# Sliding-window attention with a gated MLP on one core: the last row block stored in three pieces, the first chunk's softmax sums from one matmul, and a new order of the planned steps

## The chip, the cores and the metric

The kernel runs on one core of a Trainium2 chip. The metric is the device time of one execution in microseconds. A core has TensorE (PE, with its weight loads shown apart as PEld), VectorE (DVE), ScalarE (ACT), GpSimd (POOL) and SyncE (SP), and each engine takes its own instructions strictly in the order in which the program issued them.

## The reference

One transformer layer with pre-layernorm, sequence 2048, width 512, 32 heads of 16 columns, MLP width 1376, all in bf16:

```python
h  = x + A(layernorm(x));  h2 = h + B(layernorm(h))
# A: q,k,v = x @ wqkv;  each position s looks at s, s-2, ..., s-14 (8 places, those < 0 masked)
logits = einsum("bhsd,bhswd->bhsw", q, kg) * 16**-0.5
o = einsum("bhsw,bhswd->bhsd", softmax(logits), vg);  A = o @ wo
# B: gate = x @ W_gate; up = x @ W_up;  B = (relu(gate) * up) @ W_down
```

## The kernel before

The 2048 rows are cut into four chunks of 512 (`tk` 0 to 3), a chunk into four row blocks of 128. The work is written as 744 planned steps (`add(key, engine, ...)`). A chunk goes through these steps; the names below are the keys in the code, with the number of the part behind them:

- layernorm of x: `xst`, `xag` (statistics, DVE), `xxn` (normalised rows, on DVE or ACT), `xtp` (transposes, PE L531), `xte` (eviction, ACT L547), or a transposing DMA in place of the last two.
- q, k and v: 12 groups of four 128x512 matmuls (L572), each evicted on ACT (L580). In chunk 0 the first six groups come in pieces a, b (two matmuls of 256 columns each) and c (four).
- attention: `pr` products of q with shifted k (DVE, L620; in chunk 0 halves, L637), `sc` (16 matmuls, L628, summing over head columns), `ex` (exponent, ACT L696), in chunk 0 `mk` (masking the first columns, DVE L699). The eight places are in two halves, so there are `sc0`, `sc1`, `ex0`, `ex1`, `mk0`, `mk1`.
- softmax sums: `den` on PE, `dl` and `dr` on ACT (logarithm and exponent of its negative). In a chunk listed in `DEN1`, a DVE step `es` (L728) first adds the two halves and `den` is one matmul (L713); in the others `den` is two matmuls into one bank (L716). Chunks 1 to 3 then scale the weights (`am`, DVE L740); chunk 0 scales the result (`om`, DVE L795).
- `bd` spreads the weights over partitions by DMA from SP's queue (L756, four issues to a half), `mu` multiplies by shifted v (DVE L788, halves in chunk 0 L803), `ta` adds halves by an accumulating DMA from POOL's queue (L831), `tree2` and `tree1` add the rest (DVE L791, L825).
- `wo` output projection (L867), `rs` residual, layernorm of h (`hnm`, `hsq`, `hxn`, `htp`, `hte`).
- MLP: `mm` (up and gate, L940), evictions `ue` (L944) and `ge` (L947) on ACT, product `gu` (DVE L968), the last 96 columns apart (L907, L913, L917).
- `dn` down projection (L990), one step for `ft` 0 to 7 and one for `ft` 8 to 10; `o` adds the residual (DVE L1003, chunks 2 and 3), `os` stores (L1009; L1027 for chunks 0 and 1, whose residual is added by a DMA).

The order of the steps is written out by hand in a table `RANK`, one number for each step in the order of the `add` calls. `Plan.order` makes one queue of each engine, sorted by `RANK`, and never goes out of that order in a queue; the planner's durations only decide which buffer a step takes and in which order the engines' streams are written. So the table gives the order on each engine exactly. Buffers are few: 8 PSUM banks, 5 large tiles `big` for products, 9 tiles `quad`.

The down projection of the very last row block is cut into column pieces by `LASTC`, each with a bank, a DVE step and a store of its own; the store of the last piece listed goes through ACT's queue, the others through SP's:

```python
cs = (0,) + LASTC + (D,)
parts[-1:] = [(BPC - 1, a, b) for a, b in zip(cs, cs[1:])]
...
last = tk == NCK - 1 and n == len(parts) - 1
def f_os(j=j, c0=c0, c1=c1, ob=ob, tk=tk, q=nc.scalar if last else nc.sync):
    q.dma_start(out_rows[:, tk * BPC + j, c0:c1], ob.t[:, c0:c1])
```

Of the kernel before, what the change touches and what calls it, by code (L numbers as in the profile page):

```python
# [17 lines left out]
RANK = [  # L18
# [38 lines left out]
]  # L57


# [143 lines left out]
def kernel(  # L203
# [12 lines left out]
    Bsz, S, D = A_x.shape  # L216
# [5 lines left out]
    W = 8  # L222
    DIL = 2
    PADL = 16
    DEN1 = (1, 2, 3)
    BCD = {(0,0):"SSSS",(0,1):"SSSS",(1,0):"SSSS",(1,1):"SSSS",(2,0):"SSSS",(2,1):"SSSS",(3,0):"SSSS",(3,1):"SSSS"}
    PRE = ()
    PRD = ()
# [163 lines left out]
    HSP = ()  # L392
    TMT = (0, 1, 2, 3)
    TTM, DTG, ATE = 0.0845, 0.35, 0.3
    LASTC = (D // 2,)

    LNA = ((0, 1, 0, 1), (0, 0, 0, 0))

# [156 lines left out]
    for tk in range(NCK):  # L555
# [155 lines left out]
        def f_dn(exs=exs, dn=dn, tk=tk, es=None):  # L711
            if tk in DEN1:
                nc.tensor.matmul(dn.t[:], lhsT=(same if tk in EARLY else spread)[:], rhs=es.t[:], start=True, stop=True)  # L713
                return
            for hf in range(2):
                nc.tensor.matmul(dn.t[:], lhsT=(same if tk in EARLY else spread)[:], rhs=exs[hf].t[:], start=(hf == 0), stop=(hf == 1))  # L716
# [6 lines left out]

        if tk in DEN1:
            es = Buf(es_s)
# [250 lines left out]
        if tk == NCK - 1:  # L976
            cs = (0,) + LASTC + (D,)
            parts[-1:] = [(BPC - 1, a, b) for a, b in zip(cs, cs[1:])]
# [98 lines left out]
```

## Time and profile before

| what | value |
| --- | --- |
| three timed runs | 196.38, 196.60, 196.94 us; median 196.6 |
| the profiled execution, whole time | 196.0 us |
| its span in the trace | 193.7 us (2.3 us lie around it) |
| granted TensorE clock, mean | 1.00 |
| busy: PE, DVE, ACT, POOL | 188.5, 147.2, 115.2, 17.4 us |

The profile is of one execution, 0.6 us under the median of the timed runs. Times in its rows count from the start of the span. A line of the timeline gives start, length, engine, source line, operation, what it writes and reads, and in brackets the idle time before it and who ended it. Matmuls are pipelined, so one 128x512 matmul is shown as 379 ns long while the next starts about 216 ns after it. About one matmul record in sixty is missing; the weight loads are all there, and serve to place the steps.

### The profile page before, as it was taken

What the parts mean: (1) busy time and instruction counts of PE and PEld (TensorE: products, weight loads), DVE (VectorE), ACT (ScalarE), POOL (GpSimd) and SP (SyncE); (2) the same over time, 40 slices, a digit from 0 to 9 for tenths busy, and PEclk for the clock granted to TensorE, in tenths of its full rate; (3) what the DMA queues carried; (4) which work ended last, traced back from release to release, by engine and by line L of the source; (5) the groups of instructions that cost most, each with busy time, mean ns of one, the idle gap of its engine ahead of it and who ended that gap; (6) DMA issues with size and microseconds to landing.
All of it is one profiled execution on the core that took longest, in us unless ns stands there. A gap on an engine that the chain in (4) does not pass through costs nothing.

```text
span 193.7 us, 3083 instructions
## 1 busy us (share of the span) xinstructions
PE 188.5 (97%) x1120; PEld 99.0 (51%) x1139; DVE 147.2 (76%) x239; ACT 115.2 (59%) x241; POOL 17.4 (9%) x35
## 2 busy tenths in 40 slices
PE   7999999999999999999999999999999999999993
PEld 7986455555436435454444554444445444545452
DVE  6889999999999999999997679999564401134331
ACT  3489898965999673965156649623478712435500
POOL 3000002330000013100044001003000000000000
PEclk9999999999999999999999999999999999999999
DMA  6799564999902609917579974135101624001102
GB/s 205 242 296 376 138 155 93 192 196 260 353 5 49 171 14 199 191 33 170 122 143 194 180 192 90 29 80 94 18 0 27 162 58 135 0 27 54 30 23 86
DMA packets 25070, 24.61 MB, mean 127 GB/s; under 512 B 11136, under 2 KB 21344, under 8 KB 25056
## 3 DMA queue, kind: packets, MB, share of 16 engines
q1 hardware_dynamic: 22032, 16.23, 30.1%
q0 software_dynamic: 2304, 7.34, 20.8%
q10 hardware_dynamic: 720, 0.85, 1.2%
q8 instruction: 9, 0.15, 0.3%
q14 instruction: 5, 0.04, 0.1%
HBM read 8.42 MB, written 2.10 MB: 54 GB/s over the span
## 4 chain that ended last, share of the span: by engine, by line
PE 97%; ACT 1%; issue 1%; DVE 0%; ACTq 0%
PE bank L940 35%; PE bank L572 21%; PE bank L990 20%; PE bank L867 7%; PE bank L628 4%; PE bank L421 3%; PE bank L907 3%; PE bank L531 2%; PE bank L429 1%; ACT up_sb L944 1%; PE bank L870 0%; PE bank L713 0%; PE bank L716 0%; DVE row L1003 0%; ACT vT L580 0%
## 5 line engine op out<-in xcount | busy, mean ns | idle before, releaser
L940 PE MATMUL bank<-quad,wgu_sb 128*128 128x512 bf16 x312 | 72.4, 379 | 0.4
L940 PEld LDWEIGHTS <-wgu_sb 128*128 128x128 bf16 x320 | 31.0, 98 | 36.4 <-issue 1.0
L990 PE MATMUL bank<-wd_sb,gT 128*128 128x512 bf16 (+2 forms) x185 | 39.6, 366 | 0.1
L944 ACT CAST up_sb<-bank 128x512 bf16<-128x512 f32 x40 | 22.3, 590 | 22.2 <-PE bank L940 20.5
L572 PE MATMUL bank<-quad,wqk_sb 128*128 128x512 bf16 (+1 forms) x148 | 29.4, 344 | 0.3
L947 ACT ACTIVATE gr<-bank 128x512 bf16<-128x512 f32 x40 | 23.5, 606 | 9.5 <-PE bank L940 5.2
L968 DVE TENSOR_TENSOR gT<-gr,up_sb 128x1024 bf16<-128x1024 bf16 x20 | 13.8, 688 | 19.4 <-ACT up_sb L944 10.5
L990 PEld LDWEIGHTS <-gT 128*128 128x128 bf16 (+1 forms) x187 | 18.2, 98 | 19.8 <-DVE gT L968 0.2
L620 DVE TENSOR_TENSOR big<-quad,kT 128x4096 bf16<-128x4096 bf16 x12 | 27.2, 2284 | 0.2 <-ACT kT L580 0.2
L788 DVE TENSOR_TENSOR big<-big,vT 128x4096 bf16<-128x4096 bf16 x12 | 27.1, 2285 | 0.2 <-PE bank L940 0.2
L572 PEld LDWEIGHTS <-wqk_sb 128*128 128x128 bf16 x152 | 16.7, 113 | 10.3 <-issue 0.2
L831 POOL DMA_DIRECT2D big<-big x12 | 10.5, 904 | 81.7 <-DVE big L788 54.2
L791 DVE TENSOR_TENSOR big<-big 128x1024 bf16<-128x1024 bf16 (+2 forms) x24 | 16.9, 728 | 0.0
L572 PE MATMUL bank<-quad,wv_sb 128*128 128x512 bf16 x61 | 15.3, 380 | 0.2
L867 PE MATMUL bank<-wo_sb,quad 128*128 128x512 bf16 x62 | 15.0, 379 | 0.1
L1003 DVE TENSOR_TENSOR row<-x_sm,bank 128x512 bf16<-128x512 bf16 (+1 forms) x9 | 5.5, 627 | 12.2 <-PE bank L990 12.2
L456 ACT ACTIVATE row<-x_sm,mv 128x512 bf16<-128x512 bf16 x12 | 8.6, 718 | 7.2 <-DVE mv L448 7.1
L547 ACT COPY quad<-bank 128x1024 bf16<-128x1024 bf16 (+1 forms) x10 | 8.6, 898 | 7.2 <-PE bank L531 7.2
L878 DVE SCALAR_TENSOR_TENSOR x_sm<-x_sm,bank 128x512 bf16<-128x512 bf16 x12 | 8.2, 687 | 4.9 <-PE bank L867 4.7
L580 ACT CAST kT<-bank 128x512 bf16<-128x512 f32 x16 | 9.1, 597 | 3.3 <-PE bank L572 1.8
L467 DVE BATCH_NORM_STATS2 st<-x_sm 128x6 f32<-128x512 bf16 x16 | 10.2, 675 | 0.4 <-DMA x_sm<-in_A_x_dram 0.4
L580 ACT CAST quad<-bank 128x512 bf16<-128x512 f32 x16 | 9.5, 602 | 1.6 <-PE bank L572 1.5
(77 smaller groups left out, 169.5 us busy)
## 6 DMA issues: line engine op xcount, KB each, us to landing
big<-big POOLq DMA_DIRECT2D x12, 512.0 KB, 5.3
big<-ex SPq DMA_DIRECT2D x32, 128.0 KB, 2.8
wgu_sb<-in_B_W_gate_dram SPq DMA_DIRECT2D x2, 688.0 KB, 7.7
wgu_sb<-in_B_W_up_dram SPq DMA_DIRECT2D x2, 688.0 KB, 7.5
wd_sb<-in_B_W_down_dram SPq DMA_DIRECT2D x2, 640.0 KB, 7.9
x_sm<-in_A_x_dram SPq DMA_DIRECT2D x2, 512.0 KB, 5.1
x_sm<-up_sb POOLq DMA_DIRECT2D x4, 256.0 KB, 3.8
out_dram<-x_sm SPq DMA_DIRECT2D x4, 256.0 KB, 2.3
```

The source lines that it names most:

```text
L572: nc.tensor.matmul(mm.t[:, lo:hi], lhsT=wv_sb[:, dt, t:D:NT] if c == 2 else wqk_sb[:, dt, c * D + t:(c + 1) * D:NT], rhs=xnT.t[:, dt, lo:h ...
L580: nc.scalar.copy(out=o, in_=mm.t[:])
L620: V.tensor_tensor(out=pb.t[:].rearrange("p (t w) s -> p t w s", t=2), in0=q4, in1=k4, op=ALU.mult)
L788: V.tensor_tensor(out=mt.t[:], in0=ab.t[:], in1=v8, op=ALU.mult)
L791: V.tensor_tensor(out=mt.t[:, 0:n, :], in0=mt.t[:, 0:n, :], in1=mt.t[:, n:2 * n, :], op=ALU.add)
L831: nc.gpsimd.dma_start(mt.t[:, 0:4, :], mt.t[:, 4:8, :], accum_op=ALU.add)
L867: nc.tensor.matmul(od.t[:], lhsT=OT.t[:, t, j * P:(j + 1) * P], rhs=wo_sb[:, t, :], start=(t == 0), stop=(t == NT - 1 and tk not in RPE))
L940: nc.tensor.matmul(mm.t[:fs, lo:hi], lhsT=wgu_sb[:, dt, g, ft * P: ft * P + fs], rhs=hnT.t[:, dt, lo:hi], start=(dt == 0), stop=(dt == NT ...
L944: nc.scalar.copy(out=ub.t[:fs, i, :], in_=um.t[:fs, :])
L947: nc.scalar.activation(out=gr.t[:fs, i, :], in_=gm.t[:fs, :], func=ACT.Relu)
L968: V.tensor_tensor(out=gt.t[:fs, 0:n, :], in0=gr.t[:fs, 0:n, :], in1=ub.t[:fs, 0:n, :], op=ALU.mult)
L990: nc.tensor.matmul(od.t[:, c0:c1], lhsT=gts[ft].t[:fs, ft % 2, j * P:(j + 1) * P], rhs=wd_sb[:fs, ft, c0:c1], start=(ft == 0), stop=(ft == ...
```

## The change

Three things are changed.

1. `LASTC` goes from (256,) to (256, 384): the last row block's output is made in pieces of 256, 128 and 128 columns instead of 256 and 256. The number of planned steps rises by four (two `dn`, one `o`, one `os`).
2. `DEN1` takes in chunk 0: one DVE step `es` more, one 128x512 matmul less in `den` of chunk 0.
3. `RANK` is a new table with 749 numbers.

```diff
 RANK = [
     0, 1, 2, 3, 4, 5, 6, 7, 8, 9, 10, 11, 12, 13, 14, 15, 16, 17, 18, 19,
     20, 22, 23, 25, 29, 31, 32, 21, 24, 26, 28, 30, 36, 39, 40, 27, 33, 35, 37, 42,
-    47, 51, 34, 38, 41, 43, 46, 50, 55, 44, 56, 69, 77, 64, 65, 76, 79, 48, 53, 60,
...
+    45, 49, 34, 38, 41, 43, 46, 50, 54, 64, 73, 75, 78, 65, 67, 70, 81, 47, 56, 58,
...
-    DEN1 = (1, 2, 3)
+    DEN1 = (0, 1, 2, 3)
...
-    LASTC = (D // 2,)
+    LASTC = (D // 2, 3 * D // 4)
```

Put against the `add` calls, the two tables read as follows in the places of which the prediction speaks (chunk behind the dot; q0a is piece a of group q0; dn3a, dn3b, dn3c are the column pieces of the last row block):

```
PE, start, before: xtp0.0 fill xtp1.0 fill q0a k1a xtp2.0 q1a xtp3.0 k1b q1b q0b k2a q1c k1c ...
PE, start, after:  xtp0.0 fill xtp1.0 fill k1a xtp2.0 q1a xtp3.0 k1b q2a k2a q1b q1c k1c ...
DVE, chunk 0, before: seven half products, mk1.0, the eighth, xst.3, mk0.0, xst.2, xag.2, mu1c.0 ...
DVE, chunk 0, after:  eight half products, mk1.0, xst.3, mk0.0, xst.2, xag.2 with es.0, mu1c.0 ...
PE, up to wo1.1: the same 117 steps in both tables, den.0 shorter by one matmul after
DVE, up to tree1_1.1 (the last before wo1.1): 112 steps before; the same and es.0 after
PE, end, before: dn0lo dn1lo dn2lo dn0hi dn1hi dn2hi dn3b dn3a
PE, end, after:  dn0lo dn3b(lo) dn1lo dn0hi dn1hi dn3b(hi) dn2lo dn2hi dn3a dn3c
SP, end, before: (transpose of chunk 3) os0.3 os2.3 os1.3 os3a.3          ACT: os3b.3
SP, end, after:  (transpose of chunk 3) os1.2 os2.2 os0.2 os3b.3 os0.3 os1.0 os3.2 os1.3 os2.3 os3a.3   ACT: os3c.3
```

70 rows, old and new, of the table RANK are left out of this document.

## The prediction

> **What bounds the kernel now.** I read the head of the page first, then the chain of work that ended last, then who waited for whom.
>
> ```profile
> span 193.7 us, 3083 instructions
> ...
> PE 188.5 (97%) x1120; PEld 99.0 (51%) x1139; DVE 147.2 (76%) x239; ACT 115.2 (59%) x241; POOL 17.4 (9%) x35
> ...
> PE   7999999999999999999999999999999999999993
> ...
> DVE  6889999999999999999997679999564401134331
> ...
> PE 97%; ACT 1%; issue 1%; DVE 0%; ACTq 0%
> ```
>
> PE is busy in every slice and carries 97% of the chain. The list of waits, cut to PE, has one entry, for the first warm-up matmul:
>
> ```profile
> PE bank L421 <- DVE warm L322: 1.0, 1, 1.0
> ```
>
> So from 1.0 us to the last down projection PE never visibly stands still: the kernel is bound by PE's count of matmuls, and an order can gain nothing in this execution by filling PE's gaps. But the slices show DVE at 9 tenths from 12 us to some 100 us as well. Added up over that part:
>
> ```profile
> core 0: us, PE busy (x) PEld busy (x) DVE busy (x) ACT busy (x) POOL busy (x), PEclk, DMA share, GB/s
> ...
> sum 74.00, PE 73.44 PEld 37.80 DVE 72.91 ACT 58.46 POOL 8.03; mean PE 12.24 PEld 6.30 DVE 12.15 ACT 9.74 POOL 1.34
> ```
>
> Between 12 and 86 us DVE is idle for 1.1 us of 74, hardly more than PE. Where the two meet decides whether a saving on PE reaches the end. They meet here (timeline around 84 to 86 us):
>
> ```profile
> 83.64 0.68 DVE L968 TENSOR_TENSOR gT<-gr,up_sb 128x1024 bf16<-128x1024 bf16 x1
> ...
> 84.38 1.55 PEld L990 LDWEIGHTS <-gT 128*128 128x128 bf16 x8 [0.17 <-DVE gT L968]
> 84.54 1.89 PE L990 MATMUL bank<-wd_sb,gT 128*128 128x512 bf16 x8
> ...
> 85.63 0.43 DVE L825 TENSOR_TENSOR quad<-big 128x512 bf16<-128x512 bf16 x1
> ...
> 86.05 0.96 PEld L867 LDWEIGHTS <-quad 128*128 128x128 bf16 x5
> ...
> 86.26 1.03 PE L867 MATMUL bank<-wo_sb,quad 128*128 128x512 bf16 x4
> ```
>
> Chunk 0's first down projection loads its weights at 84.38, and the gated product it needs ends at 84.32 (83.64 + 0.68). Chunk 1's first output projection `wo1.1` loads at 86.05, and the last `tree1` ends at 86.06. PE goes straight on at 86.26, so it loses nothing yet, but its spare time there lies between 0 (by the weight load) and 0.2 us (by the matmul).
>
> **The change part by part.** *Chunk 0's softmax sums.* The two matmuls are this piece of the chain, and the price of the DVE step is read from an operation of the same shape on two 128x512 bf16 tiles and the start behind it:
>
> ```profile
> 29.48 0.43 PE bank L716 x2
> ...
> 59.78 0.42 DVE L740 TENSOR_TENSOR ex<-ex,rec 128x512 bf16<-128x512 bf16 x1 [0.34 <-ACT rec L722]
> 60.13 0.41 DVE L502 TENSOR_SCALAR row<-x_sm,mv,rs 128x512 bf16<-128x512 bf16 x1
> ```
>
> PE: one of two goes, 0.43 / 2 = 0.22 less. DVE: `es.0` adds 60.13 - 59.78 = 0.35. Behind `es.0` in DVE's queue stand the `mu` steps of chunk 0, and so everything up to 86 us.
>
> *The start.* Before, four matmuls of 256 columns stand ahead of the third block's transposes; after, two.
>
> ```profile
> 8.22 0.73 DVE L502 TENSOR_SCALAR row<-x_sm,mv,rs 128x512 bf16<-128x512 bf16 x2
> ...
> 8.46 0.60 PE L572 MATMUL bank<-quad,wqk_sb 128*128 128x256 bf16 x4
> ...
> 8.89 0.39 PE L531 MATMUL bank<-identity,row 128*128 128x128 bf16 x4
> ```
>
> PE would be at the transposes at 8.46 + 0.22 = 8.68. Their input is the first of the two L502, which ends at 8.63 (8.22 and the 0.41 that one takes above). With some 0.1 us from DVE to PE the transposes start at about 8.75, so PE loses 0.0 to 0.15; I take 0.08. The piece `k1c`, which with `q1c` releases DVE's first product, now has one piece less ahead of it (0.22) and that loss, so DVE's dense stretch starts 0.14 earlier.
>
> *The meeting at `wo1.1`.* In both tables PE's queue up to it holds the same 117 steps, and DVE's queue up to the last `tree1` the same steps with `es.0` added. So PE comes there 0.22 - 0.08 = 0.14 earlier, and DVE 0.35 - 0.14 = 0.21 later if its waits stay as they are: 0.35 to be covered by 0 to 0.2 of spare time. PE stalls 0.15 to 0.35; with shorter DVE waits, 0. I take 0.15, by the matmul row, since that is what counts on PE. PE then comes away from there at -0.14 + 0.15 = +0.01: the matmul saved is given back to DVE.
>
> *After 86 us* PE alone is the bound, and the next margins, from the rows below, are 0.35 (121.08 - 120.73) at chunk 1's down projection and 0.42 (180.73 - 180.31) at chunk 3's.
>
> ```profile
> 120.05 0.68 DVE L968 TENSOR_TENSOR gT<-gr,up_sb 128x1024 bf16<-128x1024 bf16 x1
> ...
> 121.08 0.31 PEld L990 LDWEIGHTS <-gT 128*128 128x128 bf16 x2
> ...
> 179.62 0.69 DVE L968 TENSOR_TENSOR gT<-gr,up_sb 128x1024 bf16<-128x1024 bf16 x1 [1.15 <-ACT gr L947]
> ...
> 180.73 2.47 PEld L990 LDWEIGHTS <-gT 128*128 128x128 bf16 x12
> ...
> L947 ACT ACTIVATE gr<-bank 128x512 bf16<-128x512 f32 x40 | 23.5, 606 | 9.5 <-PE bank L940 5.2
> ```
>
> In the new table the product for the first stands ahead of a long `mu`. For the second, the last gate group that it needs has three groups of four matmuls (12 x 0.216 = 2.6) between itself and the down projection, and two evictions and a product (2 x 0.61 + 0.69 = 1.9) to wait for. Both margins get wider. Cost 0.
>
> *The end.* Rows of the timeline, then of the groups by shape, the chain in order of time (start, length) and the DMA issues (KB, us to landing):
>
> ```profile
> 188.74 1.92 PE L990 MATMUL bank<-wd_sb,gT 128*128 128x256 bf16 x16
> 189.94 0.35 ACTq L1009 DMA_DIRECT2D out_dram<-row  x1
> 190.69 0.42 DVE L1003 TENSOR_TENSOR row<-x_sm,bank 128x256 bf16<-128x256 bf16 x1 [0.78 <-PE bank L990]
> 191.14 0.33 SPq L1009 DMA_DIRECT2D out_dram<-row  x1
> ...
> L1003 DVE TENSOR_TENSOR row<-x_sm,bank 128x512 bf16<-128x512 bf16 x7 | 4.6, 686 | 10.9 <-PE bank L990 10.9
> ...
> 61.05 0.89 PE bank L531 x16
> ...
> out_dram<-row ACTq DMA_DIRECT2D x1, 64.0 KB, 1.6
> out_dram<-row SPq DMA_DIRECT2D x1, 64.0 KB, 1.5
> ```
>
> A 256-column matmul costs (1.92 - 0.27) / 15 = 0.11 us, the 0.27 being the overhang of the last one. A 128-column one is bounded by 0.89 / 16 = 0.056 (transposes, each with a weight load of its own) and 0.11; I take 0.056. Before 22 x 0.11 = 2.42, after 11 x 0.11 + 22 x 0.056 = 2.44: +0.02. The last DVE step shrinks: 512 columns take 0.69, 256 take 0.42, so 128 should take 0.42 - 0.13 = 0.29: -0.13. The last store has half the bytes (saves up to 0.1) and goes by ACT's queue instead of SP's (1.6 against 1.5, costs 0.1): 0, between -0.1 and +0.1. ACT has nothing else left by then. SP now has seven stores to issue in the last 4 us, about 0.35 each, 2.5 in all; the one that it issues last (`os3a`) may go out 0.6 before the piece `dn3c` ends on DVE. Hidden.
>
> The pieces of 128 columns rest on the transposes' row. [...]
>
> The pieces' stores write rows of 256 bytes, where before they were 512. [...]
>
> *Sum:* 0.01 (PE up to 86 us, softmax sums included) + 0.02 - 0.13 + 0 = -0.10. The profiled execution took 196.0 for its 193.7 of span, and would take 195.9. The timed runs' median stands 0.6 above it at 196.6; the same difference gives 196.5.
>
> **The rivals.**
>
> *The order takes away DVE's waits, and stalls of the timed runs (faster).* For it: all three timed runs (196.38 to 196.94) lie above the profiled one, and at 84 to 86 us PE has no spare time, so any later transfer that holds DVE up stalls PE one for one. If the new order absorbs that, the 0.22 of the matmul and the 0.13 of the end come through and about 0.4 of the 0.6 goes: 196.6 - 0.35 - 0.4 = 195.85. Against it: DVE has only 1.1 us of idle time to give, and the runs' distance may be no stall at all.
>
> *DVE comes later still (slower).* In DVE's queue of chunk 0 `mk1` moves behind the eighth half product. SP's spreading of the weights waits for it, and `mu1c` waits for that:
>
> ```profile
> 20.21 0.16 DVE L699 TENSOR_TENSOR ex<-ex,mask 128x16 bf16<-128x16 bf16 x1
> 20.28 1.22 DVE L637 TENSOR_TENSOR big<-quad,kT 128x2048 bf16<-128x2048 bf16 x1
> ...
> 20.39 6.14 SPq L756 DMA_DIRECT2D big<-ex  x8
> ...
> 26.97 1.23 DVE L803 TENSOR_TENSOR big<-big,vT 128x2048 bf16<-128x2048 bf16 x1
> ...
> DMA to landing us min/median/max: 2.7/3.2/4.7
> ```
>
> A half product takes 1.1 from start to start, so the issues start 1.1 - 0.14 = 1.0 later, the fourth at about 20.39 + 3 x 0.77 + 1.0 = 23.7 (6.14 / 8 = 0.77 an issue). With the slowest landing (4.7) it is there at 28.4; the same sum for before gives 27.4, though `mu1c` ran at 26.97, so 28.0 is nearer. `mu1c` is due at 26.97 + 0.35 - 0.14 = 27.2. DVE would lose 0.8, which reaches PE at `wo1.1`: 196.5 + 0.8 = 197.3. It decides from 0.7 us of such lateness on. Against it: with the median landing (3.2) the data are there at 26.9, in time.
>
> *Narrow matmuls wait for their weights (slower).* A weight load is shown as 98 ns long, so if it is not hidden, the end costs 22 x (0.098 - 0.056) = 0.9 more: 197.4. The transposes speak against it.
>
> ```profile
> L990 PEld LDWEIGHTS <-gT 128*128 128x128 bf16 x170 | 16.6, 98 | 17.9 <-DVE gT L968 0.2
> ```
>
> **How the numbers follow.** 0.3% is 0.6 us, about what these runs can tell from no change. The forecast, 196.5 with a range of its own from 196.0 to 197.1 (0 to 0.35 of stall, 0.1 either way at the store, 0.2 of spread in the medians), has 53 in 100 and lies within 0.3%. The faster rival has 24, late DVE 18, bare weight loads 5. So faster 0.24, same 0.53, slower 0.23. The range 195.7 to 197.5 leaves out the far part of the faster rival (some 7 in 100) and of the slower ones (some 10).
>
> **What the profile after would show.** Right: PE's only wait is again the warm-up; one L713 with 0.22 in place of two L716; PE's last matmul within 0.2 us of where it was; a last L1003 of 128 columns at about 0.29; DVE busy over 98% up to `wo1.1`, whose weight load is released by DVE. Wrong: a DVE idle time of over 0.5 before the first L803; PE's wait for L825 over 0.4 at `wo1.1`, or none with DVE done well ahead of it; steps of over 0.08 between the 128-column matmuls; a last landing of over 1.8 us.

## The result, and the profile after

The change made the kernel slower by 0.7%: a median of 197.69 us (ten runs, 197.11 to 199.18) against 196.54 for the kernel before (ten runs, 195.98 to 196.94), a ratio of 1.0068 with a 95% interval of 1.0045 to 1.0090. The forecast was 196.5 with a range from 195.7 to 197.5; the case "slower by over 0.3%" had been given 0.23. The profiled execution took 197.51 for a span of 195.7 (1.8 around it; before 196.0, 193.7 and 2.3). Ratios here leave out executions over 1.5% longer than the fastest of their kernel (five of twelve in e6, four in e5), medians hold all, so the two can differ.

The page of the kernel after: busy time, slices of PE and DVE, and the chain by engine.

```profile
span 195.7 us, 3123 instructions
...
PE 188.9 (97%) x1149; PEld 98.3 (50%) x1149; DVE 147.8 (76%) x241; ACT 114.6 (59%) x241; POOL 17.0 (9%) x35
...
PE   7699999999899999999999999999999999999993
...
DVE  6699999999899989999997669999683504121432
...
PE 73%; DVE 15%; DMA 5%; issue 2%; ACT 2%; SPq 2%; DVEq 0%; ACTq 0%
```

PE's share of the chain has gone from 97% to 73%, though its busy share of the span stays at 97%: the chain now runs through DVE up to the last place where PE waits for it. The list of waits says where, cut to PE (us in total, times, longest):

```profile
PE bank L531 <- DVE row L502: 1.4, 1, 1.4
PE bank L421 <- DVE warm L322: 1.0, 1, 1.0
PE bank L867 <- ACT kT L580: 0.6, 1, 0.6
PE bank L572 <- ACT rs L480: 0.3, 1, 0.3
PE bank L867 <- DVE quad L825: 0.2, 1, 0.2
```

Before, the warm-up's entry was the only one. Four places lose time now; three of them stand in this list (the start twice), the one at 34 us in the timeline alone. The first is the start (timeline):

```profile
6.98 0.69 DVE L467 BATCH_NORM_STATS2 st<-x_sm 128x6 f32<-128x512 bf16 x1 [1.78 <-DMA x_sm<-in_A_x_dram]
...
8.04 0.40 PE L531 MATMUL bank<-identity,row 128*128 128x128 bf16 x4 [1.39 <-DVE row L502]
...
9.33 0.38 PE L572 MATMUL bank<-quad,wqk_sb 128*128 128x256 bf16 x2 [0.33 <-ACT rs L480]
```

x's third row block lands late, its statistics stand in DVE's queue ahead of the second block's normalising, and PE's first q or k matmul starts at 9.33, not at 8.46. In the kernel before, DVE's longest wait for these loads was:

```profile
DVE st L467 <- DMA x_sm<-in_A_x_dram: 0.4, 1, 0.4
```

The second is at 34 us, behind SP's queue:

```profile
25.49 2.50 SPq L756 DMA_DIRECT2D big<-ex  x4
...
28.08 5.25 SPq L520 DMA_TRANSPOSE quad<-row  x4
28.19 2.36 DVE L803 TENSOR_TENSOR big<-big,vT 128x2048 bf16<-128x2048 bf16 x2 [0.22 <-DMA big<-ex]
...
33.88 0.83 PE L531 MATMUL bank<-identity,row 128*128 128x128 bf16 x12
...
34.80 0.58 PEld L572 LDWEIGHTS <-wqk_sb 128*128 128x128 bf16 x4 [0.26 <-issue]
34.83 1.03 PE L572 MATMUL bank<-quad,wqk_sb 128*128 128x512 bf16 x4
```

By an estimate from the profile before (0.89 / 16 = 0.056 for each of 16 transposes) these twelve are done after 12 x 0.056 = 0.67, at 34.55; the next matmul starts at 34.83, a loss of 0.28. It needs chunk 3's rows, which come by the transposing DMAs, and these stand behind the spreading of the weights on SP. This profile names no releaser there (`issue`); the lists of e4 and e5 name that DMA (`quad<-row`), with 0.4 and 0.9. The kernel before issued both some 1.45 earlier; 0.87 of that is its earlier start, which moves PE as well, and about 0.6 is left for the order:

```profile
24.04 2.49 SPq L756 DMA_DIRECT2D big<-ex  x4
26.62 3.92 SPq L520 DMA_TRANSPOSE quad<-row  x3
```

The third is at 51 us, the fourth at `wo1.1`:

```profile
48.52 2.29 DVE L620 TENSOR_TENSOR big<-quad,kT 128x4096 bf16<-128x4096 bf16 x1
49.08 0.81 PE L572 MATMUL bank<-quad,wqk_sb 128*128 128x512 bf16 x3
...
50.59 0.38 PE L870 MATMUL bank<-x_sm,identity 128*128 128x512 bf16 x1
...
50.89 1.07 ACT L580 CAST kT<-bank 128x512 bf16<-128x512 f32 x2 [4.20 <-DVE big L620]
51.51 2.29 DVE L620 TENSOR_TENSOR big<-quad,kT 128x4096 bf16<-128x4096 bf16 x1 [0.71 <-ACT kT L580]
51.52 1.02 PE L867 MATMUL bank<-wo_sb,quad 128*128 128x512 bf16 x4 [0.56 <-ACT kT L580]
```

```profile
87.67 0.38 PE L867 MATMUL bank<-wo_sb,quad 128*128 128x512 bf16 x1
87.81 0.42 DVE L825 TENSOR_TENSOR quad<-big 128x512 bf16<-128x512 bf16 x1
...
88.29 0.76 PEld L867 LDWEIGHTS <-quad 128*128 128x128 bf16 x5 [0.73 <-DVE quad L825]
88.29 1.04 PE L867 MATMUL bank<-wo_sb,quad 128*128 128x512 bf16 x4 [0.24 <-DVE quad L825]
```

At 50.89 ACT evicts chunk 3's k block of t = 2 (`k2ev.3`). Its matmuls are the last ones ahead of the output projections, and its bank is full at 49.89 (49.08 + 0.81). For most of the 4.2 us that ACT stands still it waits for them; for the last 1.0 it waits for DVE's product `pr0t2.1` to end (48.52 + 2.29 = 50.81). That product reads chunk 1's part of k blocks 2 and 3 in one instruction, and from the first address to the last it spans chunk 3's part of block 2, which the eviction writes. In the table before, the matmuls of that k block stand 13 places earlier in PE's queue. With ACT held, PE gets no bank for `wo2.0` (51.52 - 50.59 - 0.22 = 0.72 lost), and DVE's next product waits 0.71 for the eviction. At `wo1.1` DVE comes late with the last `tree1`, and PE's second matmul starts at 88.29, 0.62 after the first, where the four from 88.29 on start 0.22 apart (1.04 less the 0.38 of the last, by 3): 0.40 lost. That the held eviction makes this fourth stall too is not shown: e5 and e18 below have it without the third.

From its first q or k matmul to the end of its last matmul PE takes 182.19 us before (8.46 to 190.65) and 183.18 after (9.33 to 192.51). The three stalls make 0.28 + 0.72 + 0.40 = 1.40, the matmul saved takes 0.22 off, and the end (below) adds 0.03: 1.21 for the 0.99 measured, so that 0.22 stays unexplained.

The end, in the timeline:

```profile
192.54 0.29 DVE L1003 TENSOR_TENSOR row<-x_sm,bank 128x128 bf16<-128x128 bf16 x1 [0.20 <-PE bank L990]
192.86 0.36 ACTq L1009 DMA_DIRECT2D out_dram<-row  x1
```

The DMA issues (KB each, us to landing), then the chain's last piece (start, length) in the kernel after and in the kernel before:

```profile
out_dram<-row ACTq DMA_DIRECT2D x1, 32.0 KB, 1.5
```

```profile
182.93 9.59 PE bank L990 x66
```

```profile
181.11 9.56 PE bank L990 x55
```

Eleven matmuls more cost 0.03, the last DVE step takes 0.29 in place of 0.42, and the last store lands after 1.5.

### The profile page after: what moved, and what is told of

Its sections match the earlier page's. It is cut to its first block, busy times and chain, and to the rows that moved or that the text cites. A ratio compares the mean times of both kernels' runs of the same rounds, so it can differ in the third digit from the quotient of the medians.

```text
span 195.7 us, 3123 instructions
## 1 busy us (share of the span) xinstructions
PE 188.9 (97%) x1149; PEld 98.3 (50%) x1149; DVE 147.8 (76%) x241; ACT 114.6 (59%) x241; POOL 17.0 (9%) x35
## 4 chain that ended last, share of the span: by engine, by line
PE 73%; DVE 15%; DMA 5%; issue 2%; ACT 2%; SPq 2%; DVEq 0%; ACTq 0%
PE bank L940 26%; PE bank L990 19%; PE bank L572 14%; PE bank L867 7%; DVE big L620 5%; DVE big L788 4%; PE bank L628 3%; DMA x_sm<-in_A_x_dram 3%; DVE big L791 2%; PE bank L907 2%; PE bank L531 2%; DMA big<-ex 2%; DVE gT L968 1%; SPq L756 1%; DVE quad L825 1%
## 5 line engine op out<-in xcount | busy, mean ns | idle before, releaser
L990 PE MATMUL bank<-wd_sb,gT 128*128 128x512 bf16 (+4 forms) x198 | 39.9, 356 | 0.0
L944 ACT CAST up_sb<-bank 128x512 bf16<-128x512 f32 x40 | 22.9, 597 | 16.1 <-PE bank L940 14.3
L572 PE MATMUL bank<-quad,wv_sb 128*128 128x512 bf16 x64 | 16.0, 381 | 0.0
L1003 DVE TENSOR_TENSOR row<-x_sm,bank 128x512 bf16<-128x512 bf16 (+2 forms) x10 | 5.7, 579 | 8.2 <-PE bank L990 7.9
L547 ACT COPY quad<-bank 128x1024 bf16<-128x1024 bf16 (+1 forms) x10 | 8.7, 891 | 5.3 <-PE bank L531 5.3
L502 DVE TENSOR_SCALAR row<-x_sm,mv,rs 128x512 bf16<-128x512 bf16 x24 | 8.7, 407 | 3.1 <-ACT rs L484 3.1
```

What stands on the lines that cost most here:

```text
L572: nc.tensor.matmul(mm.t[:, lo:hi], lhsT=wv_sb[:, dt, t:D:NT] if c == 2 else wqk_sb[:, dt, c * D + t:(c + 1) * D:NT], rhs=xnT.t[:, dt, lo:h ...
L944: nc.scalar.copy(out=ub.t[:fs, i, :], in_=um.t[:fs, :])
L990: nc.tensor.matmul(od.t[:, c0:c1], lhsT=gts[ft].t[:fs, ft % 2, j * P:(j + 1) * P], rhs=wd_sb[:fs, ft, c0:c1], start=(ft == 0), stop=(ft == ...
```

## The experiments

PE's part is the time from its first q or k matmul to the end of its last matmul, so that a late start doesn't count; the profiled execution alone shows it. In brackets stands the median of the kernel before, run in turn with that row's kernel; e7, e8 and e12 to e14 follow in the text.

| kernel | median us (before) | 95% interval of the ratio | PE's part | first q/k matmul |
| --- | --- | --- | --- | --- |
| before | | | 182.19 | 8.46 |
| after | 197.69 (196.54) | 1.0045 to 1.0090 | 183.18 | 9.33 |
| e1 | 198.47 (196.75) | 1.0049 to 1.0113 | 183.35 | 9.46 |
| e2 | 196.88 (196.75) | 0.9990 to 1.0044 | 183.51 | 7.93 |
| e3 | 196.34 (196.75) | 0.9950 to 1.0002 | 182.43 | 8.90 |
| e4 | 197.29 (196.75) | 0.9993 to 1.0049 | 183.67 | 8.65 |
| e5 | 197.56 (196.57) | 0.9963 to 1.0028 | 183.18 | 9.26 |
| e6 | 197.29 (196.57) | 0.9956 to 1.0013 | 181.86 | 8.26 |
| e9 | 197.15 (196.61) | 1.0006 to 1.0068 | 183.42 | 8.51 |
| e10 | 196.88 (196.61) | 1.0000 to 1.0071 | 184.35 | 8.35 |
| e11 | 196.64 (196.61) | 0.9972 to 1.0031 | 183.03 | 8.98 |
| e15 | 197.28 (196.75) | 1.0010 to 1.0074 | 183.64 | 8.75 |
| e16 | 196.55 (196.75) | 0.9969 to 1.0016 | 182.64 | 9.07 |
| e17 | 196.22 (196.71) | 0.9947 to 0.9997 | 182.44 | 8.78 |
| e18 | 197.33 (196.71) | 0.9990 to 1.0057 | 182.58 | 8.51 |

**The three parts one by one (e1 to e4).** e1 takes the new order alone, e2 the one matmul for chunk 0's sums alone, e3 the three pieces alone, e4 is the kernel after again.

```diff
 e1, from after:  DEN1 and LASTC as before; RANK: without es.0, the last row block's steps as before
 e2, from before: DEN1 = (0, 1, 2, 3); RANK: es.0 behind xag3.2
 e3, from before: LASTC = (D // 2, 3 * D // 4); RANK: the last row block's steps in the new order
```

> The new order alone: after's table without the step es of chunk 0, den of chunk 0 as two matmuls, the last row block in pieces of 256 and 256 with the end of before's table. Theory O (the order itself makes stalls: the eviction of k to the last chunk held behind a product on DVE, a late spreading of the weights): 197.3 to 198.0, ratio about 1.006 as the whole change, with PE's wait of 0.6 for ACT's L580 near 50 us again. Theory D (the softmax step on DVE, 0.35 at the place where DVE holds PE): 196.5 to 196.8. Theory S (the profiled run of after merely had late input loads): 196.5, no PE wait between 12 and 86 us.

> Before's order with chunk 0's softmax sums from one matmul, es behind the statistics of chunk 2 on DVE as in the new table. Theory O: 196.3 to 196.8, since at most 0.35 of DVE less 0.2 of spare time reaches PE and 0.22 of matmul goes. Theory D: 196.9 to 197.4, with a PE wait for L825 of over 0.3 at the first output projection of chunk 1. My prediction's step: a stall of 0.15 (0 to 0.35) there, PE's end within 0.1 of before's.

> Before's order with the last row block in 256, 128 and 128 columns and the new table's order of chunk 3's last steps. All theories: 196.4 (a tenth less), between 196.2 and 196.7; steps of 0.056 between the 128-column matmuls, the last DVE step 0.29. If narrow matmuls wait for their weights or the 256-byte rows land late: 196.9 to 197.4.

> The changed kernel once more, with a second profile. Theory O: 197.4 to 198.2, and the waits near 50 us (PE for ACT's L580) and near 70 us (DVE for the spread weights) are there again. Theory S: where the input loads land as early as in the profile of before (third block by 5.6 us), the span is within 0.5 us of before's 193.7.

The order alone gives 1.0081, and the intervals of e2 and e3 hold 1: the order carries the loss. e3's profile has no wait on PE but the warm-up's, and its time from PE's last matmul to the end of the span is 2.81, against 3.05 before. e2 saves nothing that can be measured; in its profile x's chunk 1 was late and cost PE 1.0 near 17 us, and PE has no wait for L825 in it. e1, without `es.0`, does stall at `wo1.1`, by 0.34 (88.07 to 88.63, less 0.22): the order makes that stall without `es.0` as well. e4 has the same stalls as the profile after (0.53 at 34, 0.71 at 51, 0.46 at 87 us), at a smaller distance to the kernel before; its interval, 0.9993 to 1.0049, holds 1.

**The held eviction (e5, e6).** e5 makes chunk 1's products of q and k in two instructions, one to a k block, so that none spans another chunk's columns. e6 leaves them and moves chunk 3's k block.

```diff
 e5, from after:  chunk 1's L620 in two halves: kT block t, then block t + 1
 e6, from after:
-PE: k2mm.3 where the table has it            ACT: k2ev.3 likewise
+PE: k2mm.3 behind sc1.1                      ACT: k2ev.3 behind ex1.1
```

> The changed kernel with chunk 1's products of q and k as two DVE instructions to a step, one for each column block t, instead of one over two blocks; nothing else. Theory K (the 4.2 us for which ACT stands before its L580 at 50.9 us is the eviction of k's block 2 of chunk 3 held back behind DVE's product, because that one instruction spans the rows between its two blocks): ACT's eviction starts when its matmuls end, near 49.8; PE's wait of 0.5 to 0.7 near 51.5 and DVE's of 0.7 there go; DVE pays 4 x 0.07 = 0.3 for the splits; 0.4 to 0.9 us faster than after in the same rounds. Theory B (a PSUM bank or a q buffer holds the eviction): the wait of about 4.2 stays, time as after or 0.3 more.

> The changed kernel with the projection of k's block 2 of chunk 3 moved on PE from before the first output projection to behind the second score step of chunk 1 (sc1), and its eviction on ACT from before rs0 of chunk 0 to behind ex1 of chunk 1. Theory K: PE's wait near 51.5 goes and DVE's 0.7 at the product before it, 0.6 to 1.2 us faster than after, and the wait at the first output projection of chunk 1 near 88 us shrinks from 0.4 below 0.2. Theory B: the wait comes back at another eviction, time within 0.3 of after.

Who waits for whom, first e5, then e6, cut to PE and to the evictions into kT:

```profile
ACT kT L580 <- PE bank L572: 3.2, 1, 3.2
...
PE bank L421 <- DVE warm L322: 1.0, 1, 1.0
...
PE bank L572 <- DMA quad<-row: 0.9, 1, 0.9
...
PE bank L876 <- DVE quad L834: 0.2, 1, 0.2
```

```profile
PE bank L421 <- DVE warm L322: 1.0, 1, 1.0
...
ACT kT L580 <- PE bank L572: 0.7, 1, 0.7
...
PE bank L572 <- ACT rs L480: 0.3, 1, 0.3
```

With the product split, ACT waits for PE's matmuls only and PE's wait at 51 us is gone: it is the one instruction's span over two blocks that made the dependency. In e5 the transposes of chunk 3 cost 0.9 instead, the stall at `wo1.1` is there with 0.34, PE's part is that of the kernel after, and the gain that was expected isn't shown. In e6 the stalls at 51 and at 87 us are both gone, and PE's part is the shortest of all. Its timed runs fell into two groups (195.07 to 197.46 and 198.45 to 199.03), so it was run again:

> e6's kernel a second time (the order after, chunk 3's k block of t = 2 moved behind sc1.1 and ex1.1). If the held-back eviction and what followed from it (0.72 and 0.40 on PE) are the larger part of the loss: 1.1 less than the kernel after's 197.3 to 197.7, so 196.2 to 196.6, ratio 0.998 to 1.001, and no PE wait over 0.3 between 40 and 100 us. Rival (something outside of PE's waits makes the new order slow): 197.2 or more, as the kernel after.

In e18 the wait at 51 us is absent again and PE's part is 0.6 below that of the kernel after, but the stall at `wo1.1` is there with 0.46, and the runs spread from 195.8 to 201.3. So with that k block moved PE's part is 0.6 to 1.3 shorter than in the kernel after; that moving it suffices is not shown.

**The mask and the start (e7, e8).** Both come from the kernel after.

```diff
 e7: DVE: mk1.0 ahead of the eighth half product
 e8: DVE: xxn1.0 ahead of xst2.0, xte1.0 ahead of xst3.0
```

> The changed kernel with mk1 of chunk 0 ahead of the eighth half product on DVE, as before the change. If the late spreading of the weights causes PE's wait of 0.3 to 0.5 near 34.5 us (the transposing DMAs of chunk 3 stand behind it in SP's queue), this wait falls under 0.1 and DVE's wait of 0.2 to 1.1 before its first L803 too: 0.3 to 0.8 us faster than after. If not, within 0.2 of after.

> The changed kernel with two DVE steps of the start moved up: the normalisation of row block 1 ahead of the statistics of row block 2, and the copy of block 1's transposes ahead of the statistics of block 3. Theory S (part of the time comes from DVE waiting in order for late rows of x): the first L572 starts at or before 8.6 us also where the third row block lands after 6 us; 0.3 to 0.8 us faster than after, and the spread of the runs is smaller. Otherwise within 0.2 of after.

e7: 197.89, ratio 1.0061 (1.0034 to 1.0088). Its profile caught an execution in which x's chunk 1 was 2.3 late at 19 us; the wait at 34 us is gone in it, but PE was held 2.3 ahead of that place, so this doesn't show that the mask's place causes the wait. DVE's `mk1.0` waits 1.1 for the exponent in it, which the late x may have caused. The gain of 0.3 to 0.8 that was expected did not come. e8: 198.20, 1.0088 (1.0059 to 1.0118). PE's first q or k matmul comes at 7.78, and then PE waits 0.81 for the third row block and 0.94 at 19 us: the wait only moved, and here too the expected gain did not come.

**Heads crossed (e9 to e12).** A table's first 111 or 114 steps, up to chunk 0's last product or mask, joined to the rest of the other. e11 adds e6's edit to e9; e12 is e2 and e3 together.

```diff
 e9,  after:  RANK = before's first 111 steps, then the others in after's order
 e10, before: RANK = after's first 114 steps, then the others in before's order
```

> The kernel after, with the first 111 steps (everything up to chunk 0's last half product, about the first 30 us) in the order of the kernel before, and the rest in the order of the kernel after. Theory A (the order's own waits): the start's loss of about 0.8 to 1.2 us goes (x's third row block at 5.3 to 5.7 us, first L572 near 7.2), the wait for the k eviction near 51 us (0.7) and the stall at wo1.1 (0.3 to 0.45) stay: 197.3 to 197.7 of the kernel after less 0.9, so 196.4 to 196.8. Rival B (x's lateness is luck and has nothing to do with the order): the third row block lands anywhere between 5.4 and 7.1, and the median stays at 197.3 to 197.7.

> The kernel before, with the first 114 steps (up to chunk 0's second mask) in the order of the kernel after; two matmuls for chunk 0's denominators, two pieces at the end. Theory A: x's third row block lands at 6 us or later, PE's matmuls start 0.5 to 1.2 later, nothing else changes: 196.6 + 0.9 = 197.5. Rival B: 196.6, with a start as in the kernel before or not, by luck.

> As e9, and with chunk 3's k block of t = 2 moved behind sc1.1 on PE and its eviction behind ex1.1 on ACT (as in e6). Theory A: neither the wait near 51 us nor the late start is left, and DVE, 0.7 earlier, no longer stalls PE at wo1.1: e9's time less 0.7 + 0.3, so 195.4 to 195.8, below both kernels. Rival B: no PE wait over 0.3 from 20 us on, but late x loads in most runs: median 196.5 to 197.5, spread over 2 us as in e6.

> The kernel before with both named parts and without the new order: one matmul for chunk 0's denominators (es.0 behind xag3.2 on DVE) and the last row block in three pieces. By the steps: 0.22 less on PE, 0.13 less on the last DVE step, 0.02 more on PE: 196.6 - 0.33 = 196.3. By the product of the ratios of e2 and e3 (1.0017 x 0.9976 = 0.9993): 196.45. Rival: es.0's 0.35 on DVE reaches PE at wo1.1, which costs up to 0.35: 196.6.

Against theory A, x's third row block was late in e11's profile with before's head (PE waits 1.1 for L502), and in time in e10's with after's head (first matmul at 8.35). So the head does not cause it. e9's ratio, 1.0037, lies between those of the two comparisons of the kernel after (1.0068 and 1.0021), so before's head brings nothing that these runs can tell. e11, which differs from e9 by that k block's place alone and was run in turn with it, is 0.5 below e9; its slowest run (197.04) lies below six of e9's twelve. This is the clearest evidence of what the held eviction costs. e11, and e16 below, have most of the new order and don't differ from the kernel before by more than these runs can tell. The joint adds a wait of its own in both e9 and e11 (0.7 for L547 at 23 us). e12 gave 196.23 against 196.61, 0.9991 (0.9961 to 1.0020), with 196.3 expected: without the new order the two named parts do no harm.

**POOL's closing steps (e13 to e16).** From the last packet to the end of the span the kernel after takes 1.72 us, before 1.38. POOL's last steps, first of the kernel before, then after (operation, count, duration, first and last start):

```profile
L1072 POOLq EVENT_SEMAPHORE  x2: 17/17/17, 193.5 to 193.6; - x2
L1072 POOLq DRAIN  x1: 40/40/40, 193.4 to 193.4; - x1
```

```profile
L1072 POOLq EVENT_SEMAPHORE  x2: 17/17/17, 195.5 to 195.6; - x2
L1072 POOLq DRAIN  x1: 40/40/40, 195.1 to 195.1; - x1
```

The new order gives POOL two semaphore waits more, 70 instructions in the trace instead of 68.

```diff
 e13, e14, from before:
-nc.gpsimd.memset(eps_t[:], EPS)
+nc.gpsimd.memset(eps_t[:], EPS)      # three times in e13, five times in e14
 e15, from after (e16: from e11):
-nc.gpsimd.memset(kT[:, :, 0:PADL], 0.0); nc.gpsimd.memset(vT[:, :, 0:PADL], 0.0)
+V.memset(kT[:, :, 0:PADL], 0.0); V.memset(vT[:, :, 0:PADL], 0.0)
```

> The kernel before with the line nc.gpsimd.memset(eps_t[:], EPS) three times in place of once: two more POOL instructions early on (70 in place of 68), nothing else. Theory P (from the 69th POOL instruction on, one waits 0.36 us longer, whatever it is): the last POOL DRAIN of the closing steps is followed by its event after 0.40 in place of 0.04, and the span gets 0.36 longer past the last packet (1.7 us from the last packet to the end in place of 1.4). Rival (the closing is longer because of what stands in the new order): 0.04 and 1.4 as in the kernel before.

> As e13 with five in place of one memset: 72 POOL instructions. Theory P: the 0.36 stands ahead of the 69th instruction, which here is the clearing of the semaphores, two steps earlier in the closing: 0.40 ahead of that one, 0.04 ahead of the event behind the last DRAIN; 1.7 from the last packet to the end. Rival (only the number of semaphore waits of the new order counts): 1.4.

> The kernel after, with the two clearings of kT's and vT's first 16 columns on DVE (before any of x is there) and not on POOL: 68 POOL instructions. Theory P: 0.04 behind the last DRAIN, 1.4 from the last packet to the end, so 0.36 less than the kernel after: 197.3 to 197.7 less 0.36 = 197.1 +- 0.3. The waits at 34, 51 and 87 us stay (0.28, 0.72, 0.40). Rival: 1.7, and 197.3 to 197.7.

> e11's kernel with two POOL instructions fewer as in e15. If PE's waits inside the new order and the closing are the whole loss: e11's 196.64 less 0.36 = 196.3, at least 0.3 below the kernel before in the same rounds. Rival (something else in the new order still costs): 196.6 or more, no better than e11.

The same view of e13, then of e14:

```profile
L1074 POOLq DRAIN  x2: 40/71/102, 192.7 to 193.0; - x2
L1074 POOLq EVENT_SEMAPHORE  x2: 17/17/17, 193.4 to 193.5; - x2
L1074 POOLq EVENT_SEMAPHORE_RANGE_CLEAR  x1: 139/139/139, 192.8 to 192.8; - x1
```

```profile
L1076 POOLq EVENT_SEMAPHORE  x4: 17/17/17, 193.2 to 194.2; - x4
L1076 POOLq DRAIN  x2: 40/71/102, 193.4 to 194.0; - x2
L1076 POOLq EVENT_SEMAPHORE_RANGE_CLEAR  x1: 139/139/139, 193.9 to 193.9; - x1
```

In e13 a pause stands behind the last DRAIN (193.0 to 193.4), in e14 ahead of the clearing (0.40 behind a DRAIN that ends at 193.46); in both that is ahead of the 69th instruction. e15 and e16, with 68, are back at 1.33 and 1.32. So theory P holds for the span. It holds for nothing else: the time around the span is 2.2 to 2.3 us in all nine profiles with 68 instructions and 1.7 to 1.8 in all eleven with 70 or 72. What the span gains at its end is missing around it, and no change of the kernel's time can be seen. e13, with the pause inside its span, gave 196.22 against 196.75 (0.9963 to 1.0018), e14 197.01 (0.9982 to 1.0037). Of e15's expected gain of 0.36 there is no trace against e4, and e16 came to 196.55 where 196.3 was expected. Of the span's 2.0 us more, then, 0.36 is made up for outside the span.

**The pieces again.**

> e3's kernel a second time (the order before, two matmuls for chunk 0's sums, three pieces at the end). By the steps that held (last DVE step 0.13 shorter, PE's narrow matmuls +0.03, 0.24 less from PE's last matmul to the end of the span in e3): 0.1 to 0.25 below the kernel before, ratio 0.9987 to 0.9995. Rival (e3's 0.9976 was the whole of a larger gain): 0.997 to 0.998, 0.4 to 0.6 below.

0.9972 (0.9947 to 0.9997), beside e3's 0.9976. The order before with three pieces at the end is the one version whose whole interval lies below 1. Its gain of 0.5 is more than the 0.2 that its profile accounts for; the rest stays open.

## Why the prediction was wrong

The step that failed is the one at the meeting: "In both tables PE's queue up to it holds the same 117 steps, and DVE's queue up to the last `tree1` the same steps with `es.0` added. So PE comes there 0.22 - 0.08 = 0.14 earlier". Equal numbers of steps were taken for equal waits. The steps are mixed in another way, and PE stood still for 0.28 and 0.72 ahead of that place, where the sum had no stall behind the start. With the late start (0.87) it came to `wo1.1` at 87.67, 1.41 later than before (86.26) instead of 0.14 earlier. Nothing in the profile before excluded it, and its list of waits held a warning of the same kind, an eviction into kT that waits for a product, with slack enough there to hide it:

```profile
ACT kT L580 <- DVE big L620: 1.5, 1, 1.5
```

Point by point:

- *Softmax sums, -0.22 on PE:* right; the groups of the kernel after hold no L716 and one L713 more. e12 against e17 (0.9991 and 0.9972) shows no gain from it.
- *The start, 0.08:* PE came 0.87 late in the profile. That is not the reason given, and e10 and e11 show that the new start's order is not the cause. The 0.1 us from DVE to PE in this term was the author's estimate; in the profile after the transposes' weight load starts at 8.04, 0.05 behind the end of its L502 (7.59 + 0.40).
- *Stall at `wo1.1`, 0.15 (0 to 0.35):* the place and the releaser (L825) were right, the size was 0.40, 0.46 in e4. The reason was not: e1 has 0.34 without `es.0`, and e2, with `es.0` in the order before, has none (though behind a pause of 1.0 on PE). The sum left DVE's waits as they were; between 12 and 86 us DVE's busy time fell from 72.91 to 71.94:

```profile
sum 74.00, PE 73.33 PEld 38.19 DVE 71.94 ACT 57.18 POOL 7.78; mean PE 73.33 PEld 38.19 DVE 71.94 ACT 57.18 POOL 7.78
```

- *After 86 us, 0:* right; PE has no further wait.
- *The end, +0.02 and -0.13:* +0.03 and -0.13 measured, and 0.24 in all from PE's last matmul to the end of e3's span. The last eleven matmuls, of 128 columns, start 0.055 to 0.058 apart in the profile after, where 0.056 was taken. That half the bytes save the last store up to 0.1 was the author's estimate, and whether rows of 256 bytes land late was left open in e3's expectation. The runs show one store of each kind: through ACT's queue 32 KB in rows of 256 bytes landed after 1.5, where 64 KB in rows of 512 took 1.6 before; through SP's queue 1.4 against 1.5.
- *The rival "DVE comes later still":* its first half came true. The spreading's first issue came at 22.22 instead of 20.39; less the late start of 0.87 that is 0.96, against 1.0 forecast. But `mu1c` waited 0.22 only. What was late was the work queued behind it on SP, the transposes of chunk 3, which the rival had not followed.
- *What would make it wrong:* "PE's wait for L825 over 0.4" is at its bound; "PE's only wait is again the warm-up" failed at four places.

Why the kernel after lies 1.15 above before in one comparison and 0.54 in e4's and e15's is open. The start is part of it, and it goes with the order. x's third row block is issued 1.7 us after the span's start in every profile. It landed at 5.59 in the profile before and at 6.95 in the one after; over all twenty, at 5.4 to 5.9 in the eight whose later part is in the order before (before, e2, e3, e10, e12, e13, e14, e17), and at 5.9 to 7.1 in the twelve others. The first q or k matmul came at 8.4 on average in those eight and at 8.9 in the others (without e8, whose start has an order of its own). What a later part could do to the first 9 us is not shown by any run.

## What to carry to other kernels

A new order of the same steps is not neutral until each engine's queue has been read for what each step waits for; compare who holds whom, not how many steps stand ahead. Look above all for an instruction that covers two blocks of a buffer: here it locked, from first to last address, what lies between, and a writer there held its engine (ACT, for the last 1.0 us of its 4.2). When a step is moved later, follow the queue that it releases past the first consumer, to what is queued behind.

## What the runs showed of the hardware

- POOL stands still longer ahead of its 69th instruction: 0.42 us in the profile after (195.10 to 195.52) and some 0.4 in e13, ahead of an event, and 0.40 in e14, ahead of a clearing, where 0.04 lies between the last DRAIN and its event in the profile before. The time around the span is 1.7 to 1.8 in the eleven profiles with 70 or 72 instructions on POOL and 2.2 to 2.3 in the nine with 68. No cost to the whole can be seen. A difference between spans of a few tenths is no difference of times until the part around the span has been looked at. The cause is not shown.
- Behind a pause of 1.8 us on PE its granted clock was 0.50 in e12. In the profiled execution x's chunk 1 was late (windows of 2 us: busy time of PE, PEld, DVE, ACT and POOL, then granted clock, DMA share, GB/s):

```profile
17.00:19.00 2.00, 0.58 (x3) 0.10 (x1) 2.00 (x3) 2.00 (x5) 0.00 (x0) 1.00 1.04 323
19.00:21.00 2.00, 1.58 (x23) 0.76 (x24) 2.00 (x3) 1.85 (x4) 0.00 (x0) 0.94 1.01 397
21.00:23.00 2.00, 1.78 (x14) 1.45 (x14) 2.00 (x4) 1.69 (x3) 0.00 (x0) 0.50 0.71 285
23.00:25.00 2.00, 2.00 (x11) 0.67 (x13) 2.00 (x4) 1.72 (x3) 0.00 (x0) 0.71 0.44 92
```

  The pause ends at 19.42 (PE's wait for ACT's L499). The clock was 0.94 in the two microseconds around its end, 0.50 from 21 to 23 and 0.71 from 23 to 25, and the weight loads of the 128x512 matmuls stand 0.43 apart there (22.48, 22.91, 23.34), where these matmuls stand 0.216 apart at a clock of 1.00. In e7, with a pause of 2.3, it was 0.50 from 23 to 25 as well; in e10, with one of 1.2 at the same place, 1.00 from 17 to 23. Whether the length of the pause decides is not shown by these three.
